# Two scalings spread over single steps: the Sinkhorn iteration of a three-layer kernel cut into 31 pieces, and the gates of two experts applied to their finished sums

## The chip, the cores and the metric

One core of one Trainium2 chip runs the whole program. The metric is the device time in microseconds (us) of one execution. The engines are named as the profile names them: PE is TensorE (matrix products), PEld its weight loads, DVE is VectorE, ACT is ScalarE, POOL is GpSimd, and SP is SyncE, which here only issues DMAs.

## The reference, cut to what matters

A linear attention layer gives `x` (3072 tokens of 384), a dense layer (384 to 2048 to 384) follows, and behind it a layer of 8 experts, each of which sees every token. The gates of the experts are not picked by top-k but by a Sinkhorn iteration over the whole 3072 x 8 table:

```
logits = x @ w_gate
P = exp(logits - logits.max())
for _ in range(8):
    P /= P.sum(1, keepdims=True) + 1e-09
    P /= P.sum(0, keepdims=True) + 1e-09
    P *= N / E
for e in range(E):
    h = np.maximum(x @ w1[e], 0.0)
    ye = h @ w2[e]
    out += P[:, e:e + 1] * ye
```

So no gate is known before the last token has its logits, and before 16 normalisations, each of which needs the whole table. A gate is one factor per token and expert; it may be applied to `h` or to `ye`, since the second product is linear.

## The kernel before, in words

The program has two parts. The first one (to about 771 us) holds attention, the dense layer and the first expert of one unit. The change lies at the beginning of the second part, which does the remaining work of the expert layer, and from there on all times are counted from the start of the span.

The second part works on three units of 1024 tokens, in the order 1, 2, 0. A unit passes through its experts one by one, each expert in four **steps** (`NGR = 4`) of 256 hidden columns. Unit 1 comes first and has all 8 experts, so step 0 to 3 is expert 0, step 4 to 7 is expert 1, step 8 begins expert 2. All weights and activations are split in a high and a low part, and every product is made in three passes of 128 x 512 matmuls (high x high, low x high, high x low).

**First products.** `x @ w1` of a step is done in Winograd's form: seven block products in place of eight (`TERMS`, in the order `ORDER = (0, 2, 1, 4, 3, 5, 6)`, positions k = 0 to 6). `first(s, a)` makes one of them, of 3 or 6 matmuls, in one PSUM bank, and `drain(s, a, ps)` adds it to what the others left (the tile `gt`; line 622 on DVE, but for the first one, which ACT copies, line 624). Five of the seven positions leave DVE one such sum; k = 4 leaves it two, and k = 0 none. There are only **two banks** for this, taken in turn by `next_ring`, so a first product waits until the sum of the bank's last user is done. Small results that pass through PSUM (named `sm`) take their turn in the same two banks.

**Between the products.** `weigh(s, z)` takes a finished block of `gt`. For the steps of expert 0 (`s < NGR`) ACT makes the relu, since the gates are not known yet; for later steps DVE makes relu and gate in one instruction (line 651, reading the gate tile `gp`). Then ACT makes the high part `gh`, and POOL (in unit 1) the low part `gl`.

**Second products.** `seconds(s)` makes the 36 matmuls of a step with `w2` (line 682). They are dealt out behind the first products of the next step, five behind each position, six behind the last, and add up in six banks through all experts of a unit. Expert 0 of unit 1 is kept apart: at its end `o_first` multiplies the six banks by the gate on DVE (line 697) and stores them to DRAM (`y0g`), to be added when the unit ends. So a step has 33 + 36 = 69 matmuls.

**Weights.** `make1` and `make2` convert the weights of a later step: four small sums on DVE, two copies on ACT, four subtractions on POOL, and DMAs.

**Sinkhorn.** The table `P` is the tile `lg`, 128 x 24 x 8. Row sums lie within a partition; column sums need a product with a matrix of ones on PE (line 377). The iteration is a list `sinks` of 11 entries, and three are called in each of the steps 0 to 2 (positions 1, 3, 5) and two in step 3 (positions 0, 2). A middle entry, `sink_next`, holds the PE product and all nine DVE instructions that follow it. The list is in hand-written order: what `side[k]` holds is issued behind the sum at position k and ahead of the five second products there.

**The first gates.** `gate_first` makes the gates of experts 0 and 1 of unit 1 without DRAM: eight ACT instructions put a gate column on a diagonal, two PE products with ones spread it over the partitions (line 582, the tile `pb`), and ACT copies it to `gp` (line 583). This is done at the end of step 3 and in step 4. `gate_out` writes all gates to DRAM (`ped`), and `gate_load` brings one expert's gates of a unit as a 128 x 1024 tile; there are two such tiles.

Of the kernel before, what the change touches and what calls it, by code (L numbers as in the profile page):

```python
# [8 lines left out]
F32 = mybir.dt.float32  # L9
# [12 lines left out]
E, F = 8, 1024  # L22
NTOK = B * S
# [61 lines left out]
def delta_mish_sinkhorn_kernel(  # L85
# [16 lines left out]
    nc = tc.nc  # L102
# [242 lines left out]
    P = lg  # L345
    Pf = lg.rearrange("p t e -> p (t e)")

    def sink_max():
        nc.vector.tensor_reduce(out=sk["m"][:, 0:1], in_=Pf, axis=AX.X, op=ALU.max)

    def sink_max_all():
        ps = small[0]()
        nc.tensor.transpose(ps[0:1, 0:128], sk["m"][:, 0:1], id_sb)
        nc.vector.tensor_reduce(out=sk["m"][0:1, 1:2], in_=ps[0:1, 0:128], axis=AX.X, op=ALU.max, negate=True)

    def sink_start():
        m2, m3 = sk["m"][0:1, 1:2], sk["m"][:, 2:3]
        ps2 = small[0]()[:, 0:1]
        mm(ps2, lhsT=sk["ones"][0:1, :], rhs=m2, start=True, stop=True)
        nc.vector.tensor_copy(m3, ps2)  # L360
        nc.scalar.activation(out=Pf, in_=Pf, func=AF.Sigmoid, bias=m3)
        d = sk["d"]
        nc.vector.tensor_scalar(out=d, in0=Pf, scalar1=-1.0, scalar2=1.0, op0=ALU.mult, op1=ALU.add)
        nc.vector.reciprocal(out=d, in_=d)
        nc.vector.tensor_tensor(out=Pf, in0=Pf, in1=d, op=ALU.mult)

    def sink_round():
        rs = sk["rs"]
        nc.vector.tensor_reduce(out=rs, in_=P, axis=AX.X, op=ALU.add)
        nc.vector.tensor_scalar(out=rs, in0=rs, scalar1=1e-9, scalar2=None, op0=ALU.add)  # L370
        nc.vector.reciprocal(out=rs, in_=rs)
        nc.vector.tensor_tensor(out=P, in0=P, in1=rs[:, :, None].to_broadcast([128, NT, E]), op=ALU.mult)
        nc.vector.tensor_reduce(out=sk["cs"], in_=P.rearrange("p t e -> p e t"), axis=AX.X, op=ALU.add)

    def sink_round_end():
        ps = small[0]()[:, 0:E]
        mm(ps, lhsT=sk["ones"], rhs=sk["cs"], start=True, stop=True)
        cr = sk["cr"]
        nc.vector.tensor_scalar(out=cr, in0=ps, scalar1=1e-9, scalar2=None, op0=ALU.add)
        nc.vector.reciprocal(out=cr, in_=cr)  # L380
        nc.vector.tensor_scalar(out=cr, in0=cr, scalar1=float(NTOK) / E, scalar2=None, op0=ALU.mult)
        nc.vector.tensor_tensor(out=P, in0=P, in1=cr[:, None, :].to_broadcast([128, NT, E]), op=ALU.mult)


    def sink_first():
        sink_start()
        sink_round()

    def sink_next():
        sink_round_end()  # L390
        sink_round()
# [150 lines left out]
    def gate_out():  # L542

        q = gq2[0]
        nc.scalar.activation(
            out=q[:, 0].rearrange("p (e t) -> p e t", e=E), in_=P.rearrange("p t e -> p e t"), func=AF.Copy
        )

        def turn():
            ps = small[0]()  # L550
            for a in range(2):
                nc.tensor.transpose(ps[0:96, a * 128:a * 128 + 128], q[:, 0, a * 96:a * 96 + 96], id_sb)
            rows = q[0:96, 1:3].rearrange("p a x -> p (a x)")[:, 0:256]
            nc.scalar.activation(out=rows, in_=ps[0:96, 0:256], func=AF.Copy)
            for a in range(2):
                nc.sync.dma_start(out=pe_dram[0][96 * a:96 * a + 96, :], in_=rows[:, 128 * a:128 * a + 128])

        return turn
# [9 lines left out]
    def gate_first():  # L568

        a = pool2[1, "x"].tile([128, 1024], F32, tag="x", name="gd")  # L570
        for e in range(2):
            pbs[U0, e] = pool2["p"].tile([128, 1024], F32, tag="p", name="gp")

        def diagonal(e):
            for t in range(8):
                nc.scalar.activation(
                    out=a[:, 128 * t:128 * t + 128], in_=id_sb, func=AF.Copy, scale=P[:, 8 * U0 + t, e:e + 1]
                )

        def spread_out(e, i):  # L580
            ps = next_ring("pb")
            mm(ps, lhsT=sk["ones"], rhs=a[:, 512 * i:512 * i + 512], start=True, stop=True)
            nc.scalar.activation(out=pbs[U0, e][:, 512 * i:512 * i + 512], in_=ps, func=AF.Copy)

        return diagonal, spread_out
# [1034 lines left out]
    with tc.manual_schedule():  # L1620
# [5 lines left out]
        for s in range(N + 1):  # L1626
# [18 lines left out]
            if s == NGR - 1:  # L1645
                diagonal, spread_out = gate_first()
                side[3].append(lambda: diagonal(1))
                for i in range(2):
                    side[5 + i].append(lambda i=i: spread_out(1, i))
            if s == NGR:  # L1650
                side[0].append(lambda: diagonal(0))
                for i in range(2):
                    side[1 + i].append(lambda i=i: spread_out(0, i))
                turn = []
                side[3].append(lambda: turn.append(gate_out()))
                side[5].append(lambda: turn[0]())
# [9 lines left out]
            if s > NGR and g == 1 and s + NGR - 1 < N:  # L1666
# [98 lines left out]
```

## Time and profile before

| what | value |
|---|---|
| median of 3 runs | 2259.17 us (2255.65 to 2260.9) |
| the profiled execution: its own time | 2261.18 us |
| its span, first to last instruction | 2259.2 us |
| mean granted PE clock | 0.972 of full speed |
| PE busy | 2185.5 us (97%) |
| DVE, ACT, POOL busy | 1408.2, 678.8, 680.1 us |

The page cuts the span in 40 slices of 56.5 us and gives for each the busy share of every engine in tenths, and the PE clock that the throttle granted, in tenths of full speed. One looks for slices in which a digit is lower than its neighbours, and then asks the trace for that stretch.

### The profile page before, as it was taken

To read this page: it belongs to the slowest core of one execution; us is meant where nothing else is said; L and a number is where in the kernel's file an instruction comes from. 1 tells how busy PE (TensorE), PEld (TensorE's weight loads), DVE (VectorE), ACT (ScalarE), POOL (GpSimd) and SP (SyncE) were. 2 spreads that over 40 slices of the span, in tenths; PEclk is the share of its full clock that TensorE was granted. 3 is DMA by queue.
4 is the path that set the end of the run, shared out by engine and by line. 5 is a ranking of instruction groups with operands and counts; after the bars stand their busy time and mean duration, and the time that the engine had idled before them with its cause. 6 is when DMAs were issued, how large, how long until landed. Compare 5 with 4: busy or idle time off the path is not lost.

```text
span 2259.2 us, 34766 instructions
## 1 busy us (share of the span) xinstructions
PE 2185.5 (97%) x14146; PEld 1801.7 (80%) x14146; DVE 1408.2 (62%) x2270; ACT 678.8 (30%) x1197; POOL 680.1 (30%) x532
## 2 busy tenths in 40 slices
PE   7788899999999989999999999999999999999998
PEld 6667788888888767888888888888888888888887
DVE  8894726373821376777777766666666666666665
ACT  6452332333333433333333322121121121211111
POOL 4504441435324546787786710000000000000000
PEclk7699999999999989999999999999999999999999
DMA  6385733544446325546556444444434444344342
GB/s 182 132 292 183 242 114 137 190 163 151 141 141 218 145 103 207 208 169 220 195 183 214 154 135 147 147 157 137 158 129 142 158 149 158 128 152 147 133 149 70
DMA packets 122222, 366.14 MB, mean 162 GB/s; under 512 B 9680, under 2 KB 50960, under 8 KB 121936
## 3 DMA queue, kind: packets, MB, share of 16 engines
q1 hardware_dynamic: 122064, 363.94, 47.5%
q8 instruction: 111, 1.82, 0.3%
q14 instruction: 47, 0.39, 0.1%
HBM read 271.53 MB, written 92.37 MB: 161 GB/s over the span
## 4 chain that ended last, share of the span: by engine, by line
PE 85%; DVE 10%; issue 2%; POOL 1%; ACT 1%; DMA 0%; SPq 0%; DVEq 0%; POOLq 0%; ACTq 0%
PE s L682 33%; PE b L615 30%; PE psh L310 8%; PE x L1263 7%; DVE t L1045 2%; DVE lane L1051 1%; PE y L334 1%; PE psa L982 1%; PE psa L1121 1%; DVE lane L1015 1%; PE psa L1285 1%; PE psa L1177 1%; DVE us L838 1%; PE psa L1087 1%; PE psa L1101 1%
## 5 line engine op out<-in xcount | busy, mean ns | idle before, releaser
L615 PE MATMUL b<-gx,gw 128*128 128x512 f32 x3036 | 798.0, 391 | 6.4 <-DVE gt L622 6.3
L622 DVE TENSOR_TENSOR gt<-b,gt 128x512 f32<-128x512 f32 x644 | 436.1, 689 | 443.6 <-PE b L615 421.1
L615 PEld LDWEIGHTS b<-gx,gw 128*128 128x128 f32 x3036 | 569.9, 188 | 127.0 <-DVE gt L622 8.1
L682 PE MATMUL s<-gh,gw 128*128 128x512 f32 x2208 | 624.0, 391 | 0.1
L657 ACT ACTIVATE gh<-gt 128x512 fp32r<-128x512 f32 x368 | 232.8, 633 | 971.0 <-DVE gt L651 969.9
L682 PEld LDWEIGHTS s<-gh,gw 128*128 128x128 f32 x2208 | 415.2, 188 | 88.4 <-issue 1.2
L682 PE MATMUL s<-gl,gw 128*128 128x512 f32 x1104 | 327.6, 392 | 0.0
L651 DVE SCALAR_TENSOR_TENSOR gt<-gt,gp 128x512 f32<-128x512 f32 x352 | 301.8, 857 | 4.9
L682 PEld LDWEIGHTS s<-gl,gw 128*128 128x128 f32 x1104 | 208.0, 189 | 43.5 <-issue 0.7
L310 PE MATMUL psh<-xh,w 128*128 128x512 f32 x672 | 224.0, 416 | 10.5 <-DVE gl L1252 8.2
L660 POOL TENSOR_TENSOR gl<-gt,gh 128x512 fp32r<-128x512 f32 x128 | 188.5, 1479 | 100.8 <-ACT gh L657 96.5
L660 DVE TENSOR_TENSOR gl<-gt,gh 128x512 fp32r<-128x512 f32 x240 | 164.6, 686 | 38.0 <-ACT gh L657 37.9
L1252 POOL TENSOR_TENSOR gl<-x,gh 128x512 fp32r<-128x512 f32 x80 | 103.1, 1289 | 261.0 <-ACT gh L1250 237.1
L310 PEld LDWEIGHTS psh<-xh,w 128*128 128x128 f32 x672 | 126.7, 196 | 43.2 <-DVE gl L1252 11.8
L1263 PE MATMUL x<-gh,w 128*128 128x512 f32 x576 | 153.0, 402 | 0.0
L540 POOL TENSOR_TENSOR gx<-gxr,gx 128x768 fp32r<-128x768 f32 x18 | 33.4, 1856 | 350.1 <-ACT gx L539 350.1
L471 POOL TENSOR_TENSOR gw<-gr,gw 128x640 fp32r<-128x640 f32 x70 | 116.1, 1661 | 68.7 <-ACT gw L481 68.7
L310 PE MATMUL psh<-xl,w 128*128 128x512 f32 x336 | 136.3, 406 | 0.4 <-DVE xl L838 0.4
L1263 PEld LDWEIGHTS x<-gh,w 128*128 128x128 f32 x576 | 109.0, 192 | 24.1 <-issue 1.4
L1244 ACT ACTIVATE x<-psh 128x512 f32<-128x512 f32 x80 | 47.9, 599 | 144.8 <-PE psh L310 138.8
L1263 PE MATMUL x<-gl,w 128*128 128x512 f32 x288 | 82.9, 397 | 1.0 <-POOL gl L1252 1.0
L310 PEld LDWEIGHTS psh<-xl,w 128*128 128x128 f32 x336 | 66.0, 196 | 16.1 <-DVE xl L838 1.3
(200 smaller groups left out, 2101.3 us busy)
## 6 DMA issues: line engine op xcount, KB each, us to landing
gw<-wg SPq DMA_DIRECT2D x57, 1280.0 KB, 8.4
w<-wd SPq DMA_DIRECT2D x88, 768.0 KB, 4.5
gw<-wg SPq DMA_DIRECT2D x57, 768.0 KB, 5.4
wg<-gw SPq DMA_DIRECT2D x29, 1280.0 KB, 6.0
wg<-gw SPq DMA_DIRECT2D x29, 768.0 KB, 5.1
wd<-w SPq DMA_DIRECT2D x24, 768.0 KB, 5.5
gr<-in_w_dram SPq DMA_DIRECT2D x35, 384.0 KB, 3.2
raw<-in_w_dram SPq DMA_DIRECT2D x35, 384.0 KB, 3.6
```

Source lines behind the costliest of these rows:

```text
L310: mm(ps, lhsT=wi(u, pw, kc), rhs=(xh, xl)[px][:, kc, :], start=(n == 0), stop=(n == 3 * KD - 1))
L471: nc.gpsimd.tensor_tensor(out=w[:, 1, lo:hi], in0=r, in1=w[:, 0, lo:hi].bitcast(F32), op=ALU.subtract)
L615: mm(ps, lhsT=w[:, pw, i * 128:i * 128 + 128], rhs=x[:, px, j, :], start=(n == 0), stop=(n == last))
L622: add = lambda o, i: nc.vector.tensor_tensor(out=t[:, o], in0=ps, in1=t[:, i], op=ALU.add)
L651: nc.vector.scalar_tensor_tensor(out=t, in0=t, scalar=0.0, in1=pbs[u, e][:, o:o + 512], op0=ALU.max, op1=ALU.mult)
L657: nc.scalar.activation(out=h, in_=t, func=AF.Copy)
L660: return lambda: eng.tensor_tensor(out=l, in0=t, in1=h.bitcast(F32), op=ALU.subtract)
L682: mm(o[3 * half + d], lhsT=w[:, pw, at:at + 128], rhs=hids[s, z][ph], start=(start and new and n == 0), stop=(end and not new and n == 2))
L1045: eng[0].tensor_tensor(out=slot[0], in0=lane[:, s + 1:32, s:s + 1].to_broadcast([128, n, s]), in1=lane[:, s:s + 1, 0:s].to_broadcast([128, ...
L1244: nc.scalar.activation(out=mi_x[u % 2], in_=hps.pop(u), func=AF.Mish)
L1252: eng.tensor_tensor(out=l, in0=p, in1=h.bitcast(F32), op=ALU.subtract)
L1263: mm(x2ps[c][k], lhsT=wo(u, pw, k * 128, k * 128 + 128), rhs=(h, l)[pg], start=(f == 0 and n == 0), stop=(f == U1 - 1 and n == 2))
```

## The change

The Sinkhorn list has 31 entries, each a pair: a PE part or nothing, and a part for DVE or ACT. One entry is called behind each first product, but for position 4 (which has two sums) and the very first position. The PE part is issued right behind the first product, ahead of its sum; the other part right behind the sum. A round is three entries: row sums, column sums, scaling.

The gates of experts 0 and 1 of unit 1 are no longer made by diagonals. The relu of the steps 0 to 7 is made by ACT. At the end of expert 0 the six banks are copied as they are to a tile `y2` (`o_plain`); in step 7 six DVE products apply gate 0 to it (`y_gate`); at the end of expert 1 its six banks are multiplied by gate 1 (`o_weighed`); in step 9 six DVE sums put both together (`y_sum`), and the result is stored to `y0g`. The gate tiles of both experts come from DRAM behind the last Sinkhorn entries, in step 5, and the gate of expert 2 is loaded in step 7. The loads and sums of the next unit's activations (`x_fetch`, `x_sums`, `x_split`) are placed 5 and 3 steps later in a unit.

```diff
+    def pe_columns():
+        held[:] = [small[0]()]
+        mm(held[0][:, 0:E], lhsT=sk["ones"], rhs=sk["cs"], start=True, stop=True)
...
-    sinks = deque([sink_max, sink_max_all, sink_first] + [sink_next] * (ROUNDS - 1) + [sink_round_end])
+    sinks = deque(
+        [(None, sink_max), (pe_max, sink_max_all), (pe_spread, sink_start), (None, sink_odds), (None, sink_odds_end)]
+        + [(None, sink_rows), (None, sink_columns), (pe_columns, sink_scale)] * ROUNDS
+    )
...
+    def gate_store():
+        rows = gq2[0][0:96, 1:3].rearrange("p a x -> p (a x)")[:, 0:256]
+        nc.scalar.activation(out=rows, in_=held[0][0:96, 0:256], func=AF.Copy)
+        for a in range(2):
+            nc.sync.dma_start(out=pe_dram[0][96 * a:96 * a + 96, :], in_=rows[:, 128 * a:128 * a + 128])
+        for e in range(2):
+            gate_load(U0, e)
+
+    sinks.extend([(None, gate_copy), (pe_gates, gate_store)])
...
-        if s < NGR:
+        if s < 2 * NGR:
             nc.scalar.activation(out=t, in_=t, func=AF.Relu)
...
-        start, end = s == begin2[u] or s == NGR, s == end2[u] or s == NGR - 1
+        start, end = s == begin2[u] or s in (NGR, 2 * NGR), s == end2[u] or s in (NGR - 1, 2 * NGR - 1)
...
-        o, put = os[u], o_first if s == NGR - 1 else o_out
+        o, put = os[u], {NGR - 1: o_plain, 2 * NGR - 1: o_weighed}.get(s, o_out)
...
+    def o_plain(u, half):
+        if not y2:
+            y2.append(pool2[1, "x"].tile([128, 2, KD, 1024], F32, tag="x", name="gy"))
         c = slice(512 * half, 512 * half + 512)
         for d in range(KD):
-            nc.vector.tensor_tensor(out=fin["y"][:, d, c], in0=os[u][3 * half + d], in1=pbs[u, 0][:, c], op=ALU.mult)
-        nc.sync.dma_start(out=y0g[0][:, :, c], in_=fin["y"][:, :, c])
+            if d == 1:
+                nc.vector.tensor_copy(y2[0][:, 0, d, c], os[u][3 * half + d])
+            else:
+                nc.scalar.activation(out=y2[0][:, 0, d, c], in_=os[u][3 * half + d], func=AF.Copy)
+
+    def y_gate(half, d):
+        c = slice(512 * half, 512 * half + 512)
+        tt(out=y2[0][:, 0, d, c], in0=y2[0][:, 0, d, c], in1=pbs[U0, 0][:, c], op=ALU.mult)
+
+    def o_weighed(u, half):
+        c = slice(512 * half, 512 * half + 512)
+        for d in range(KD):
+            tt(out=y2[0][:, 1, d, c], in0=os[u][3 * half + d], in1=pbs[u, 1][:, c], op=ALU.mult)
+
+    def y_sum(half, d):
+        c = slice(512 * half, 512 * half + 512)
+        tt(out=y2[0][:, 0, d, c], in0=y2[0][:, 0, d, c], in1=y2[0][:, 1, d, c], op=ALU.add)
+        if d == KD - 1:
+            nc.sync.dma_start(out=y0g[0][:, :, c], in_=y2[0][:, 0, :, c])
...
-            if s < NGR:
-                for k in (0, 2) if s == NGR - 1 else (1, 3, 5):
-                    side[k].append(sink_step)
...
+            if s in (2 * NGR - 1, 2 * NGR + 1):
+                fn = y_gate if s < 2 * NGR else y_sum
+                for half in range(2):
+                    for d in range(KD):
+                        side[(KD * half + d) // 2].append(lambda fn=fn, half=half, d=d: fn(half, d))
+                if s < 2 * NGR:
+                    side[3].append(lambda: gate_load(U0, 2))
...
-                    b = 6 + 10 * q
+                    b = 11 + 8 * q
...
-                z = drain(s, a, first(s, a))
+                ps = first(s, a)
+                item = sinks.popleft() if sinks and (s or k) and k != 4 else (None, None)
+                if item[0]:
+                    item[0]()
+                z = drain(s, a, ps)
+                if item[1]:
+                    item[1]()
```

In the order of instructions three places show it. The first is PE in step 1, around the first Sinkhorn product with ones (`sm`); `b` is the bank of a first product, `s` the banks of the second products. Before:

```order
L682 MATMUL s_7784<-gh,gw_7117 128x512
L615 MATMUL b_7800<-gx,gw_7118 128x512 x3
L377 MATMUL sm<-gate 128x8
L682 MATMUL s_7785<-gh,gw_7117 128x512
L682 MATMUL s_7783<-gl,gw_7117 128x512
```

After the change:

```order
L669 MATMUL s_7781<-gh,gw_7117 128x512
L602 MATMUL b_7810<-gx,gw_7118 128x512 x6
L389 MATMUL sm<-gate 128x8
L669 MATMUL s_7782<-gh,gw_7117 128x512
L669 MATMUL s_7783<-gh,gw_7117 128x512
```

The product with ones moved one position back, behind the first product of six matmuls at k = 2.

The second place is DVE in the same step, between two sums (`gt<-b`). Before, one sum is followed by all nine instructions of a `sink_next` and then by the next sum:

```order
L622 TENSOR_TENSOR gt<-b_7800,gt 128x512
L379 TENSOR_SCALAR gate<-sm 128x8
L380 RECIPROCAL gate<-gate 128x8
L381 TENSOR_SCALAR gate<-gate 128x8
L382 TENSOR_TENSOR lg<-lg,gate 128x192
L369 TENSOR_REDUCE gate<-lg 128x24
L370 TENSOR_SCALAR gate<-gate 128x24
L371 RECIPROCAL gate<-gate 128x24
L372 TENSOR_TENSOR lg<-lg,gate 128x192
L373 TENSOR_REDUCE gate<-lg 128x8
L622 TENSOR_TENSOR gt<-b_7821,gt 128x512
```

After the change the same nine kinds stand in three groups; here the last two of a round, with the sums of k = 1, 2 and 3 around them and two weight sums (`gr`) behind:

```order
L609 TENSOR_TENSOR gt<-b_7798,gt 128x512
L384 TENSOR_TENSOR lg<-lg,gate 128x192
L385 TENSOR_REDUCE gate<-lg 128x8
L609 TENSOR_TENSOR gt<-b_7810,gt 128x512
L393 TENSOR_SCALAR gate<-sm 128x8
L394 RECIPROCAL gate<-gate 128x8
L395 TENSOR_SCALAR gate<-gate 128x8
L396 TENSOR_TENSOR lg<-lg,gate 128x192
L494 TENSOR_TENSOR gr<-gr 128x128
L495 TENSOR_TENSOR gr<-gr 128x256
L609 TENSOR_TENSOR gt<-b_7835,gt 128x512
```

At most four Sinkhorn instructions now stand between two sums.

The third place is DVE from the end of step 8 through position 3 of step 9. Before (a gated block, an activation sum `gxr`, then the sums of k = 1 and 2):

```order
L651 SCALAR_TENSOR_TENSOR gt<-gt,gp 128x512
L531 TENSOR_TENSOR gxr<-gxr 128x256
L622 TENSOR_TENSOR gt<-b_8900,gt 128x512
L622 TENSOR_TENSOR gt<-b_8914,gt 128x512
L651 SCALAR_TENSOR_TENSOR gt<-gt,gp 128x512
L490 TENSOR_TENSOR gr<-gr 128x128
L491 TENSOR_TENSOR gr<-gr 128x256
L622 TENSOR_TENSOR gt<-b_8933,gt 128x512
```

After the change, from the three products that empty the second half of expert 1's banks:

```order
L698 TENSOR_TENSOR gy<-s_8356,gp 128x512
L698 TENSOR_TENSOR gy<-s_8357,gp 128x512
L698 TENSOR_TENSOR gy<-s_8358,gp 128x512
L702 TENSOR_TENSOR gy<-gy 128x512 x2
L609 TENSOR_TENSOR gt<-b_8885,gt 128x512
L702 TENSOR_TENSOR gy<-gy 128x512 x2
L609 TENSOR_TENSOR gt<-b_8902,gt 128x512
L638 SCALAR_TENSOR_TENSOR gt<-gt,gp 128x512
L702 TENSOR_TENSOR gy<-gy 128x512 x2
L494 TENSOR_TENSOR gr<-gr 128x128
L495 TENSOR_TENSOR gr<-gr 128x256
L609 TENSOR_TENSOR gt<-b_8924,gt 128x512
```

Nine more instructions of 128 x 512 stand there, ahead of the sum of position 3.

## Rows read from the trace of the kernel before

**Rows 1.** The page: the granted PE clock in 40 slices.
```profile
PEclk7699999999999989999999999999999999999999
```
**Rows 2.** What PE waited for, 771 to 875 us: total, times, longest.
```profile
PE b L615 <- DVE gt L622: 6.3, 4, 4.2
PE sm L377 <- DVE gt L622: 3.7, 3, 2.2
```
**Rows 3.** Busy time by engine in steps 1, 3, 4, 6 and 8.
```profile
core 0: us, PE busy (x) PEld busy (x) DVE busy (x) ACT busy (x) POOL busy (x), PEclk, DMA share, GB/s
784.06:809.65 25.59, 19.99 (x76) 15.36 (x75) 17.56 (x43) 8.14 (x12) 7.76 (x6) 0.87 0.00 1
...
831.17:853.19 22.02, 19.86 (x79) 15.24 (x77) 13.06 (x29) 11.33 (x22) 11.78 (x10) 0.92 0.41 150
853.19:871.24 18.05, 18.01 (x76) 13.71 (x75) 10.12 (x17) 9.12 (x20) 8.85 (x7) 1.00 0.39 140
886.88:902.52 15.64, 15.64 (x70) 12.95 (x69) 11.01 (x16) 5.03 (x7) 10.97 (x9) 1.00 0.79 269
918.16:933.80 15.64, 15.64 (x70) 12.96 (x69) 12.89 (x17) 5.03 (x7) 11.08 (x9) 1.00 0.52 185
```
**Rows 4.** PE in order of time, around the starts of steps 1 and 5.
```profile
782.57 2.33 PE L615 MATMUL b<-gx,gw 128*128 128x512 f32 x9 [0.42 <-DVE gt L622]
...
790.20 1.12 PE L615 MATMUL b<-gx,gw 128*128 128x512 f32 x3 [4.16 <-DVE gt L622]
...
871.24 0.84 PE L615 MATMUL b<-gx,gw 128*128 128x512 f32 x3
```
**Rows 5.** A stretch of 2 us behind that wait; columns as in Rows 3.
```profile
792.00:794.00 2.00, 2.00 (x6) 1.71 (x7) 1.86 (x6) 0.00 (x0) 0.82 (x1) 0.50 0.00 0
```
**Rows 6.** The chain that ended last, pieces between 838 and 870 us.
```profile
840.63 0.12 PE sm L377 x2
840.75 1.26 PE s L682 x5
...
843.39 1.13 PE s L682 x5
...
847.70 0.86 PE pb L582 x2
...
867.26 0.22 PE sm L552 x2
```
**Rows 7.** DVE in order of time: Sinkhorn rounds beside POOL, and alone.
```profile
806.15 0.16 DVE L379 TENSOR_SCALAR gate<-sm 128x8 f32<-128x8 f32 x1
...
807.23 1.40 DVE L382 TENSOR_TENSOR lg<-lg,gate 128x192 f32<-128x192 f32 x1
...
811.97 0.68 DVE L622 TENSOR_TENSOR gt<-b,gt 128x512 f32<-128x512 f32 x1
...
822.30 0.16 DVE L379 TENSOR_SCALAR gate<-sm 128x8 f32<-128x8 f32 x1
...
822.93 0.36 DVE L382 TENSOR_TENSOR lg<-lg,gate 128x192 f32<-128x192 f32 x1
...
825.09 0.28 DVE L492 TENSOR_TENSOR gr<-gr 128x128 f32<-128x128 f32 x1
```
**Rows 8.** POOL in order of time, the same stretch.
```profile
807.12 1.30 POOL L660 TENSOR_TENSOR gl<-gt,gh 128x512 fp32r<-128x512 f32 x1
```
**Rows 9.** Groups by shape, 871 to 1262 us: busy us, mean ns.
```profile
L651 DVE SCALAR_TENSOR_TENSOR gt<-gt,gp 128x512 f32<-128x512 f32 x100 | 119.2, 1192 | 2.6
...
L697 DVE TENSOR_TENSOR gy<-s,gp 128x512 f32<-128x512 f32 x3 | 1.9, 676 | 0.0
```
**Rows 10.** Gate tiles by DMA: us from issue to landing, min, median, max.
```profile
DMA to landing us min/median/max: 4.0/9.0/10.5
```
**Rows 11.** ACT in order of time: the gate table's copy.
```profile
862.19 0.56 ACT L545 ACTIVATE gq<-lg 128x192 f32<-128x192 f32 x1
```

More of the change, by code (lines that the diff above doesn't have):

```diff
@@ L346, in delta_mish_sinkhorn_kernel, with pe_max @@
     Pf = lg.rearrange("p t e -> p (t e)")
+    rs, d = sk["rs"], lambda: sk["d"]
+    held = []
+    tt, ts1 = nc.vector.tensor_tensor, nc.vector.tensor_scalar
     def sink_max():
         nc.vector.tensor_reduce(out=sk["m"][:, 0:1], in_=Pf, axis=AX.X, op=ALU.max)
+    def pe_max():
+        held[:] = [small[0]()]
+        nc.tensor.transpose(held[0][0:1, 0:128], sk["m"][:, 0:1], id_sb)
     def sink_max_all():
-        ps = small[0]()
-        nc.tensor.transpose(ps[0:1, 0:128], sk["m"][:, 0:1], id_sb)
@@ L354, in sink_max_all, with pe_spread @@
-        nc.vector.tensor_reduce(out=sk["m"][0:1, 1:2], in_=ps[0:1, 0:128], axis=AX.X, op=ALU.max, negate=True)
+        nc.vector.tensor_reduce(out=sk["m"][0:1, 1:2], in_=held[0][0:1, 0:128], axis=AX.X, op=ALU.max, negate=True)
+    def pe_spread():
+        held[:] = [small[0]()]
+        mm(held[0][:, 0:1], lhsT=sk["ones"][0:1, :], rhs=sk["m"][0:1, 1:2], start=True, stop=True)
     def sink_start():
-        m2, m3 = sk["m"][0:1, 1:2], sk["m"][:, 2:3]
-        ps2 = small[0]()[:, 0:1]
-        mm(ps2, lhsT=sk["ones"][0:1, :], rhs=m2, start=True, stop=True)
@@ L360, in sink_start, with sink_odds @@
-        nc.vector.tensor_copy(m3, ps2)
+        m3 = sk["m"][:, 2:3]
+        nc.vector.tensor_copy(m3, held[0][:, 0:1])
         nc.scalar.activation(out=Pf, in_=Pf, func=AF.Sigmoid, bias=m3)
[L362 to L368, printed above, removed]
+    def sink_odds():
+        ts1(out=d(), in0=Pf, scalar1=-1.0, scalar2=1.0, op0=ALU.mult, op1=ALU.add)
+        nc.vector.reciprocal(out=d(), in_=d())
@@ L369, in sink_round, with sink_odds_end, sink_rows, sink_columns @@
+    def sink_odds_end():
+        tt(out=Pf, in0=Pf, in1=d(), op=ALU.mult)
+    def sink_rows():
         nc.vector.tensor_reduce(out=rs, in_=P, axis=AX.X, op=ALU.add)
-        nc.vector.tensor_scalar(out=rs, in0=rs, scalar1=1e-9, scalar2=None, op0=ALU.add)
+        ts1(out=rs, in0=rs, scalar1=1e-9, scalar2=None, op0=ALU.add)
         nc.vector.reciprocal(out=rs, in_=rs)
-        nc.vector.tensor_tensor(out=P, in0=P, in1=rs[:, :, None].to_broadcast([128, NT, E]), op=ALU.mult)
+    def sink_columns():
+        tt(out=P, in0=P, in1=rs[:, :, None].to_broadcast([128, NT, E]), op=ALU.mult)
@@ L373, in sink_round, with sink_scale @@
         nc.vector.tensor_reduce(out=sk["cs"], in_=P.rearrange("p t e -> p e t"), axis=AX.X, op=ALU.add)
-    def sink_round_end():
-        ps = small[0]()[:, 0:E]
-        mm(ps, lhsT=sk["ones"], rhs=sk["cs"], start=True, stop=True)
+    def pe_columns():
+        held[:] = [small[0]()]
+        mm(held[0][:, 0:E], lhsT=sk["ones"], rhs=sk["cs"], start=True, stop=True)
+    def sink_scale():
         cr = sk["cr"]
-        nc.vector.tensor_scalar(out=cr, in0=ps, scalar1=1e-9, scalar2=None, op0=ALU.add)
+        ts1(out=cr, in0=held[0][:, 0:E], scalar1=1e-9, scalar2=None, op0=ALU.add)
@@ L380, in sink_round_end @@
         nc.vector.reciprocal(out=cr, in_=cr)
[L381 to L391, printed above, removed]
-    sinks = deque([sink_max, sink_max_all, sink_first] + [sink_next] * (ROUNDS - 1) + [sink_round_end])
-    def sink_step():
-        if sinks:
-            sinks.popleft()()
+        ts1(out=cr, in0=cr, scalar1=float(NTOK) / E, scalar2=None, op0=ALU.mult)
@@ L400, in delta_mish_sinkhorn_kernel @@
+        tt(out=P, in0=P, in1=cr[:, None, :].to_broadcast([128, NT, E]), op=ALU.mult)
+    sinks = deque(
+        [(None, sink_max), (pe_max, sink_max_all), (pe_spread, sink_start), (None, sink_odds), (None, sink_odds_end)]
+        + [(None, sink_rows), (None, sink_columns), (pe_columns, sink_scale)] * ROUNDS
+    )
     NGR = U2 // 2
@@ L540, in x_split, with gate_copy, pe_gates @@
         nc.gpsimd.tensor_tensor(out=x[:, 1, s, o], in0=r[:, s], in1=x[:, 0, s, o].bitcast(F32), op=ALU.subtract)
-    def gate_out():
-        q = gq2[0]
+    def gate_copy():
         nc.scalar.activation(
-            out=q[:, 0].rearrange("p (e t) -> p e t", e=E), in_=P.rearrange("p t e -> p e t"), func=AF.Copy
+            out=gq2[0][:, 0].rearrange("p (e t) -> p e t", e=E), in_=P.rearrange("p t e -> p e t"), func=AF.Copy
         )
[L549 to L558, printed above, removed]
+    def pe_gates():
+        held[:] = [small[0]()]
+        for a in range(2):
+            nc.tensor.transpose(held[0][0:96, a * 128:a * 128 + 128], gq2[0][:, 0, a * 96:a * 96 + 96], id_sb)
+    def gate_store():
+        rows = gq2[0][0:96, 1:3].rearrange("p a x -> p (a x)")[:, 0:256]
+        nc.scalar.activation(out=rows, in_=held[0][0:96, 0:256], func=AF.Copy)
+        for a in range(2):
+            nc.sync.dma_start(out=pe_dram[0][96 * a:96 * a + 96, :], in_=rows[:, 128 * a:128 * a + 128])
+        for e in range(2):
+            gate_load(U0, e)
+    sinks.extend([(None, gate_copy), (pe_gates, gate_store)])
     def gate_load(u, e):
@@ L566, in gate_load @@
         pbs[u, e] = pb
[L568 to L585, printed above, removed]
     ring, ringn = [], [0]
@@ L690, in delta_mish_sinkhorn_kernel @@
     fin, slot = {}, [0]
-    def o_first(u, half):
-        if half not in fin and not fin:
-            fin["y"] = pool2[1, "x"].tile([128, KD, 1024], F32, tag="x", name="gy")
+    y2 = []
+    def o_plain(u, half):
+        if not y2:
+            y2.append(pool2[1, "x"].tile([128, 2, KD, 1024], F32, tag="x", name="gy"))
         c = slice(512 * half, 512 * half + 512)
         for d in range(KD):
-            nc.vector.tensor_tensor(out=fin["y"][:, d, c], in0=os[u][3 * half + d], in1=pbs[u, 0][:, c], op=ALU.mult)
-        nc.sync.dma_start(out=y0g[0][:, :, c], in_=fin["y"][:, :, c])
+            if d == 1:
[14 more added lines that the diff above has]
+            nc.sync.dma_start(out=y0g[0][:, :, c], in_=y2[0][:, 0, :, c])
     def o_open(u):
@@ L1641, in delta_mish_sinkhorn_kernel @@
             side = {k: [] for k in range(7)}
-            if s < NGR:
-                for k in (0, 2) if s == NGR - 1 else (1, 3, 5):
-                    side[k].append(sink_step)
[L1645 to L1656, printed above, removed]
+            if s in (2 * NGR - 1, 2 * NGR + 1):
[5 more added lines that the diff above has]
+                    side[3].append(lambda: gate_load(U0, 2))
             for n, make, lo, hi in ((s + 2, make1, 0, NW1), (s + 1, make2, NW1, GW)):
@@ L1665, in delta_mish_sinkhorn_kernel @@
                     side[1 - (make is make2)].append(lambda n=n, lo=lo, hi=hi: again(n, lo, hi))
-            if s > NGR and g == 1 and s + NGR - 1 < N:
+            if s > 2 * NGR and g == 1 and s + NGR - 1 < N:
                 side[5].append(lambda: gate_load(*plan[s + NGR - 1][0:2]))
```

## The prediction

> **What bounds the kernel now.** The first view is the profile page's line of the granted clock [rows 1]. From slice 3 on every slice shows 9 but one, slice 15, about 790 to 847 us: there the second part begins, and there PE waits long enough to lose its clock. The view of waits says for whom: 6.3 us of first products and 3.7 us of Sinkhorn products wait for DVE's sums [rows 2]. The table by step shows what a step is worth. Step 6 takes 15.64 us with PE busy all of it, so a step's 69 matmuls cost 15.64/69 = 0.227 us each, and DVE is busy for 11.01 us of it. Steps 1, 3 and 4 take 25.59, 22.02 and 18.05 us [rows 3]. Step 5 begins at 871.24 us; step 1 begins with the seventh of the nine matmuls at 782.57, at 784.06 [rows 4]. The four steps of the Sinkhorn iteration thus take 871.24 - 784.06 = 87.18 us where 4 x 15.64 = 62.56 would do: **24.6 us are there to be had**. Everything else of the second part is bound by PE.
>
> Where do the 24.6 us go? PE idles 25.59 - 19.99 = 5.6 us in step 1 and 2.2 in step 3 [rows 3]; the longest wait is 4.16 us [rows 4], and the stretch behind it runs at a granted clock of 0.50, the lower of the two levels, 1.2 GHz [rows 5]. A mean clock of 0.87 over 25.59 us costs 3.3 us, one of 0.92 over 22.02 costs 1.8 [rows 3]. Four spreads `pb` take 0.86 us each, 3.4 in all; a Sinkhorn product takes 0.12 us and makes the five matmuls behind it last 1.26 in place of 1.13, so 0.25 each, 2.0 for eight [rows 6]. The cause of the waits is one queue: nine DVE instructions stand ahead of the next sum, with two banks for the first products. They last 825.09 - 822.30 = 2.8 us alone, but 811.97 - 806.15 = 5.8 us beside a busy POOL [rows 7].
>
> **The change, part by part.**
>
> *Sinkhorn in pieces.* Two rounds per step stay, in steps 1 to 4. Take position 1 and 2. Behind the three matmuls of k = 1 come the sum (0.68 us [rows 7]) and the two column instructions, a good quarter of the round's 2.8, some 0.8 us. PE asks for their result 5 + 6 matmuls later, 11 x 0.227 = 2.5 us; 0.9 us are left over. The next first product needs the sum of k = 2: PE gets there 0.25 + 1.13 = 1.4 us later, the sum needs 0.7. So both waits vanish while DVE's instructions run at their own length, and the new order costs only its two products, 0.5 us per step.
>
> They don't always run at their own length. Instruction L382 takes 0.36 us alone and 1.40 us when a POOL subtraction runs from 807.12 for 1.30 us; it ends just behind it [rows 7, 8]. DVE's load is the check: step 6 less its four gated blocks (ACT makes the relu now) is 11.01 - 4 x 1.19 = 6.2 us [rows 3, 9], and two rounds are 5.6 to 11.6. That is 11.8 to 17.8 us in a step of 15.64 + 0.5 = 16.1. Between the ends POOL decides, which is busy for 10.97 of 15.64 us [rows 3]; at the middle, 14.8, DVE keeps up on the whole. I take 0.25 us per step for a product with ones that comes a little late, bounds 0 and 1.7. Steps 1 to 4: 4 x (15.64 + 0.5 + 0.25) = 65.6 us, against 87.18: **21.6 us gained**.
>
> The relu moves 4 ACT instructions per step into steps 4 to 7; ACT is busy for 5.03 us of 15.64 [rows 3], so this is hidden by two thirds of the step.
>
> *Step 0* does the same work before and after, with the two small products one position later or earlier; DVE's waits there stay of one kind. I take no change, bounds plus and minus 1 us.
>
> *The spreads* are gone with their 16 diagonals (counted in the 87.18). In their place the two gate transposes of 0.22 us [rows 6] move to position 1 of step 5, where they wait for the gate table's copy, 0.56 us on ACT [rows 11], which now stands behind two of the bank copies and the copy of the step's first product. PE reaches it 2.5 us into the step; I take 0.7 us of wait, bounds 0 and 1.5. **0.9 us lost.** The bank copies themselves have the cover that `o_first` has now: PE needs the first half's banks 9 second products and 9 first ones later, 4 us, for copies on two engines.
>
> *The gate loads.* SP waits for the table's store before it issues two loads, and the conversions' DMAs wait behind; the weights they bring are needed a step later. The loads land in 4.0 to 10.5 us [rows 10], with nearly two steps to `y_gate`. The gate of expert 2 is tighter: its tile is free when `y_gate` ends, about 10 us into step 7, and 9.0 us later it has landed, 3.4 us into step 8; the first gated block wants it at about 6. With 10.5 it is 5. I take 0; where it comes later than about 8, PE waits for what is over.
>
> *Step 7* has six `y_gate`. Not one like it (two SBUF inputs, 128 x 512) is in the trace; between L697 from PSUM, 0.68, and the gated blocks, 1.19 [rows 9], they are 4.1 to 7.1 us. DVE: 6.2 + 7.1 = 13.3 of 15.64 at most. Six of them and two weight sums stand ahead of the sum of k = 3, which has less than 3 us of slack: 0.5 us, bounds 0 and 1.5.
>
> *Step 8* empties expert 1's banks as step 4 did expert 0's, and has the load of 12.89 us that step 8 has now without loss [rows 3]. 0.
>
> *Step 9* is the worst: 11.01 us, three bank products of 0.68 and six `y_sum` of 0.68 to 1.19 are 17.1 to 20.2 us in 15.64. Nearly all of the new work lies ahead of the sum of k = 3. The excess is 1.5 to 4.5 us, and where PE gets most of it as one wait, the clock may fall behind it as it fell behind the 4.16 us. I take 3.0, bounds 1 and 6.5. What the step is late, the next ones give back to DVE, whose load is 11 again.
>
> Here a rule of the Trainium skill speaks against the change. The page "SBUF — State Buffer", section "SBUF: two separate sides", says that VectorE and GpSimd share a pair of ports as an exclusive lock, held for the whole instruction, which a DVE instruction with two SBUF inputs must have. L382 agrees: 1.40 us beside POOL's 1.30. By that rule step 9 would need POOL's 10.97 and ten locked DVE instructions of 0.68 one behind the other, 17.8 us, 2.1 over the step; with that in place of the 3.0 the sum below would be 18.1.
>
> *The activation sums* move out of steps 7 to 10; a step with one of them loses nothing now (step 8, 15.64 us [rows 3]). 0.
>
> **The sum.** 21.6 - 0.9 - 0.5 - 3.0 = **17.2 us**. The profiled execution took 2261.18 us, so the same after the change is 2244.0; the median of the runs is 2.0 us lower, and **2242 us** is what I predict for it.
>
> **The rivals.**
>
> *Nothing waits.* If POOL's and DVE's instructions happen to miss each other, steps 1 to 4 take 64.6 us, and steps 5, 7 and 9 lose about 1.5: 21 us, 2238. For it: a round alone is 2.8 us. Against it: POOL's 10.97 us per step.
>
> *The lock makes DVE the bound.* Rounds of 5.8 us throughout: 17.8 us per step, 6.8 us lost in steps 1 to 4, step 9 at its upper end with the clock (6.5), step 7 at 1.5, step 5 at 0.9: 22.6 - 15.7 = 7 us, 2252. For it: four instructions of each round take the slow form when POOL has a backlog. Against it: the two forms share the rounds of the trace, and the load there was the same.
>
> *Slower: the product with ones.* It stands in PE's in-order queue twice per step, ahead of five or six second products that need nothing from it. If the column sums come late by w in each of 8 rounds, PE idles 8w, and the clock loses about as much again (5.6 us idle and 3.3 us of clock in step 1). The gain of 22.6 - 4.4 = 18.2 is gone at w = 1.4 us with w x 0.6 of clock; at w = 2.2 us the waits cost 28 us, 10 more than the gain, 2269. Against it: 0.9 us of slack in each, and one lock costs 1.0.
>
> **How the numbers follow.** Forecast 0.68, by itself 2238 to 2247; nothing waits 0.14; DVE the bound 0.13; slower 0.05. The range from 2236 to 2250 leaves out the slower case, the upper half of the DVE case and little at the lower end. What a measurement of this kernel can tell from no change is about 0.2%, 4.5 us (the three runs spread over 5.3): faster 0.92, same 0.04 (the worst of the DVE case and the edge of the slower one), slower 0.04.
>
> **What would show it.** Right: slice 15 of the clock at 9; steps 1 to 4 at 16.0 to 16.8 us each; the waits for DVE's sums down from 10 us to 3 or less up to step 5; step 9 at 17 to 20 us with the wait at position 4 or 5, behind k = 3's sum. Wrong: Sinkhorn products that wait in most rounds for the column sums, a granted clock of 0.5 anywhere in steps 1 to 4, a wait in step 8 for the gate's DMA, or step 9 at 15.64.

## The result and the profile after

The changed kernel takes 2238.4 us (median of 4 runs, 2237.6 to 2240.5) where the kernel before took 2260.0 beside it. The ratio is 0.9905 (95% interval 0.9883 to 0.9927), a gain of 21.6 us. The prediction was 2242 us, the range 2236 to 2250.

The granted clock on the profile page of the changed kernel, 40 slices, answers to [rows 1]:

```profile
PEclk8699999999999999999999999999999999999999
```

Slice 15 is at 9 now. What PE waited for from 764 to 960 us (steps 0 to 9; total, times, longest) answers to [rows 2]:

```profile
PE b L602 <- DVE gt L609: 3.1, 4, 1.6
PE sm L389 <- DVE gate L385: 1.0, 4, 0.2
```

The busy time by step, steps 1 to 6 and 9, answers to [rows 3]; its columns are the same:

```profile
777.67:794.37 16.70, 16.47 (x74) 13.31 (x74) 13.95 (x31) 8.40 (x13) 9.82 (x8) 1.00 0.00 0
794.37:811.22 16.85, 16.61 (x75) 13.25 (x73) 14.21 (x30) 7.48 (x12) 10.24 (x9) 1.00 0.47 173
811.22:828.08 16.86, 16.62 (x75) 13.25 (x73) 14.22 (x30) 7.56 (x12) 10.25 (x9) 1.00 0.46 173
828.08:844.91 16.83, 16.59 (x74) 13.24 (x73) 14.21 (x31) 8.03 (x13) 10.25 (x9) 1.00 0.48 171
844.91:861.15 16.24, 16.10 (x72) 13.04 (x71) 7.41 (x14) 8.96 (x16) 10.01 (x9) 1.00 0.76 249
861.15:876.79 15.64, 15.64 (x70) 12.96 (x69) 6.45 (x12) 7.44 (x12) 10.14 (x9) 1.00 0.50 184
908.07:926.30 18.23, 16.23 (x71) 12.80 (x69) 18.05 (x27) 5.03 (x7) 11.95 (x8) 1.00 0.68 245
```

Steps 1 to 4 take 67.2 us in place of 87.2, at the full clock throughout. Behind them step 5 is 0.6 us longer than a bare step (15.64), and step 9 is the only long one: DVE is busy for 18.05 of its 18.23 us. There PE waits twice, for the sums of positions 1 and 3, in its order of time:

```profile
914.79 1.65 PE L602 MATMUL b<-gx,gw 128*128 128x512 f32 x6 [0.44 <-DVE gt L609]
...
920.95 1.65 PE L602 MATMUL b<-gx,gw 128*128 128x512 f32 x6 [1.56 <-DVE gt L609]
```

**Two gains, not one.** Step 0 of the kernel before starts at 771.63 us of its profiled execution and step 10 at 949.44: 177.8 us. In the changed kernel PE's order of time shows, for the first matmuls of steps 0 and 10:

```profile
764.98 0.62 PE L602 MATMUL b<-gx,gw 128*128 128x512 f32 x2
...
926.30 0.84 PE L602 MATMUL b<-gx,gw 128*128 128x512 f32 x3
```

That is 161.3 us, **16.5 us less**. The spans differ by 2259.2 - 2235.7 = 23.5. Of this, 771.6 - 765.0 = 6.6 us lie ahead of step 0, in code that the change doesn't touch, and 0.4 behind step 10. What those 6.6 us are is the first question of the experiments.

### The profile page after: what moved, and what is told of

The parts are those of the page before. It is cut to its first block, busy times and chain, and to the rows that moved or that the text cites. A ratio compares the mean times of both kernels' runs of the same rounds, so it can differ in the third digit from the quotient of the medians.

```text
span 2235.7 us, 34754 instructions
## 1 busy us (share of the span) xinstructions
PE 2171.5 (97%) x14138; PEld 1792.3 (80%) x14138; DVE 1399.6 (63%) x2268; ACT 684.3 (31%) x1197; POOL 680.4 (30%) x532
## 4 chain that ended last, share of the span: by engine, by line
PE 86%; DVE 10%; issue 1%; POOL 1%; ACT 1%; DMA 0%; SPq 0%; DVEq 0%; POOLq 0%; ACTq 0%
PE s L669 33%; PE b L602 30%; PE psh L310 8%; PE x L1269 7%; DVE t L1051 2%; DVE lane L1057 2%; PE y L334 1%; PE psa L988 1%; PE psa L1127 1%; PE psa L1291 1%; DVE lane L1021 1%; PE psa L1183 1%; PE psa L1149 1%; DVE us L844 1%; PE psa L1093 1%
## 5 line engine op out<-in xcount | busy, mean ns | idle before, releaser
L638 DVE SCALAR_TENSOR_TENSOR gt<-gt,gp 128x512 f32<-128x512 f32 x336 | 274.9, 818 | 4.5
L310 PEld LDWEIGHTS psh<-xl,w 128*128 128x128 f32 x336 | 65.6, 195 | 16.2 <-DVE xl L844 1.3
```

What stands on the lines that cost most here:

```text
L310: mm(ps, lhsT=wi(u, pw, kc), rhs=(xh, xl)[px][:, kc, :], start=(n == 0), stop=(n == 3 * KD - 1))
L638: nc.vector.scalar_tensor_tensor(out=t, in0=t, scalar=0.0, in1=pbs[u, e][:, o:o + 512], op0=ALU.max, op1=ALU.mult)
```

## The experiments

But for the activation loads and sums, which now come in later steps, the change lies in steps 0 to 10, and behind these all traces agree to 0.5 us. So each run is read by step from its trace: from the start of step 0 to that of step 10 before takes 177.8 us and the changed kernel 161.3.

**The kernel before, again.** No edit.

> The kernel before, unchanged, for its first part. In the two profiles the second part began at 771.6 us (before) and 765.0 us (after), though no line of the first part changed. If that is chance of the execution (the granted clock of the first 300 us), this third profile may begin its second part anywhere between 764 and 773 us. If it belongs to the program, it begins within 1 us of 771.6. From the first matmul of step 0 to the first one of step 10 both expect 177.8 us, as in the profile of before (949.4 - 771.6).

The start of its second part, in PE's order of time:

```profile
777.77 0.61 PE L615 MATMUL b<-gx,gw 128*128 128x512 f32 x2
```

So 6 us later than in the first profile of the same kernel, and from there to step 10 it takes 177.5 us. Over the eleven profiles of this study (both kernels twice, seven variants; the first part is the same in all) step 0 starts between 764.0 and 780.0 us, and the steps agree to 0.3 us wherever their code does. That range is wider than the 764 to 773 us that were expected of chance, but the same kernel shows both 771.6 and 777.8: the 6.6 us ahead of step 0 are chance of the execution.

**One part undone: Sinkhorn in its old groups.** The gates stay as in the change.

```diff
-    sinks = deque(
-        [(None, sink_max), (pe_max, sink_max_all), (pe_spread, sink_start), (None, sink_odds), (None, sink_odds_end)]
-        + [(None, sink_rows), (None, sink_columns), (pe_columns, sink_scale)] * ROUNDS
-    )
+    start = [pe_spread, sink_start, sink_odds, sink_odds_end, sink_rows, sink_columns]
+    middle = [pe_columns, sink_scale, sink_rows, sink_columns]
+    groups = deque([[sink_max], [pe_max, sink_max_all], start] + [middle] * (ROUNDS - 1) + [[pe_columns, sink_scale]])
...
+            if s < NGR:
+                for k in (0, 2) if s == NGR - 1 else (1, 3, 5):
+                    side[k].append(group_step)
```

> The changed kernel with one part undone: Sinkhorn again in 11 groups in steps 0 to 3, at the old places, while the gates are applied as in the change. Theory (the queue of nine instructions ahead of the next sum): the waits return, step 1 about 25.6 us, step 2 about 21.5, step 3 about 20.3 (22.0 without its two spreads of 0.86), step 4 back at 15.7; from the start of step 0 to that of step 5 about 95 us where the change has 79.9, a time near 2254 us. Rival (the gain came from the spreads, the diagonals and the gated blocks that left DVE): within 4 us of the change, 84 us at most for that stretch.

Busy time by step, steps 1 to 5:

```profile
785.13:810.70 25.57, 20.05 (x76) 15.36 (x76) 17.58 (x43) 8.17 (x12) 7.83 (x6) 0.87 0.00 1
810.70:832.15 21.45, 18.81 (x76) 14.59 (x75) 17.45 (x39) 7.33 (x11) 10.20 (x9) 0.92 0.37 135
832.15:852.35 20.20, 18.02 (x75) 14.45 (x73) 13.11 (x29) 7.92 (x12) 11.56 (x10) 0.92 0.39 144
852.35:867.99 15.64, 15.64 (x71) 12.95 (x69) 6.68 (x13) 8.41 (x14) 9.89 (x9) 1.00 0.52 184
867.99:884.39 16.40, 16.11 (x72) 13.03 (x71) 6.72 (x12) 9.11 (x16) 10.19 (x9) 1.00 0.74 247
```

All steps are where the theory put them, waits and half clock with them; the run's 2261.6 us, where about 2254 were expected, holds a late start of the second part, 772.75. Steps 0 to 9 take 176.8 us. So the pieces are worth 176.8 - 161.3 = 15.5 us, 8.9 of them in step 1, and everything done to the gates 177.8 - 176.8 = 1.0: the spreads give back 4.2 (1.8 in step 3, 2.4 in step 4), steps 5 and 9 take 3.4, and the rest is 0.1 in steps 1 and 2, and rounding.

**What the 1.2 us over a bare step are.** Two kernels ask it. The first leaves out the eight products with ones:

```diff
-        ts1(out=cr, in0=held[0][:, 0:E], scalar1=1e-9, scalar2=None, op0=ALU.add)
+        ts1(out=cr, in0=sk["cs"], scalar1=1e-9, scalar2=None, op0=ALU.add)
...
-        + [(None, sink_rows), (None, sink_columns), (pe_columns, sink_scale)] * ROUNDS
+        + [(None, sink_rows), (None, sink_columns), (None, sink_scale)] * ROUNDS
```

> The changed kernel without the eight products with ones: the scaling reads the column sums of its own partition, so the sum over partitions is left out. Steps 1 to 4 take 16.84 us in the change, 1.2 over the 15.64 of a bare step. Theory: all of it is the products, their own cost and their wait for late column sums, so these steps fall to 15.64 to 15.8 us, 4.5 us in all. Rival (DVE as the bound, sums late for their banks): the steps stay above 16.3 us, since DVE's work is the same.

Steps 1 to 4 take 15.70, 15.64, 15.64 and 15.64 us. Step 2:

```profile
795.76:811.40 15.64, 15.64 (x71) 12.95 (x69) 13.64 (x30) 7.50 (x12) 10.35 (x9) 1.00 0.50 185
```

With nearly the same DVE work, and POOL as busy, the sums are never late for their banks. (Step 5 takes 17.0: PE now comes to the transposes of the gate table sooner than the table is copied, and waits 0.9 us for ACT.)

The second leaves POOL idle:

```diff
+        if NS2 <= n < 8:
+            return
...
+        if s < 6:
+            hids[s, z] = h, h
+            return lambda: None
```

> The changed kernel with POOL idle in steps 0 to 5: the low parts of the activations there aren't made (the high part is used in their place) and the low parts of the weights of steps 3 to 7 are left as they were. Theory (POOL holds up the column multiplication, which takes 1.1 to 1.4 us in place of 0.36, and so the product with ones comes late): the multiplication takes 0.36 us in all rounds and steps 1 to 4 fall from 16.84 to 16.1 to 16.3 us; what stays is the products' own cost of 0.25 us each. Rival (the product's cost is its own, whatever POOL does): the steps stay at 16.7 to 16.9 us.

The busy time of step 3, and DVE's order of time in step 2 (the sum of position 5, the column multiplication, the column sum):

```profile
817.71:833.84 16.13, 16.13 (x74) 13.40 (x73) 10.40 (x30) 7.55 (x12) 0.00 (x0) 1.00 0.49 179
```

```profile
813.81 0.69 DVE L611 TENSOR_TENSOR gt<-b,gt 128x512 f32<-128x512 f32 x1 [1.14 <-PE b L604]
814.42 0.35 DVE L384 TENSOR_TENSOR lg<-lg,gate 128x192 f32<-128x192 f32 x1
814.80 0.54 DVE L385 TENSOR_REDUCE gate<-lg 128x8 f32<-128x192 f32 x1
```

The same place in the changed kernel, DVE, POOL and PE:

```profile
806.88 0.69 DVE L609 TENSOR_TENSOR gt<-b,gt 128x512 f32<-128x512 f32 x1 [1.19 <-PE b L602]
807.49 1.43 DVE L384 TENSOR_TENSOR lg<-lg,gate 128x192 f32<-128x192 f32 x1
808.95 0.51 DVE L385 TENSOR_REDUCE gate<-lg 128x8 f32<-128x192 f32 x1
```

```profile
807.41 1.30 POOL L647 TENSOR_TENSOR gl<-gt,gh 128x512 fp32r<-128x512 f32 x1
```

```profile
807.76 1.52 PE L602 MATMUL b<-gx,gw 128*128 128x512 f32 x6
809.52 0.39 PE L389 MATMUL sm<-gate 128*128 128x8 f32 x2 [0.24 <-DVE gate L385]
809.76 0.93 PE L669 MATMUL s<-gh,gw 128*128 128x512 f32 x3
```

In the second round of each step, this one, the column multiplication meets POOL's subtraction and takes 1.43 us in place of 0.35; the column sum ends at 809.46, and PE, through with its six matmuls at 807.76 + 6 x 0.227 = 809.12, waits for it. The first round of step 2, DVE and PE, is late too, by too little for the view of waits:

```profile
797.74 1.12 DVE L384 TENSOR_TENSOR lg<-lg,gate 128x192 f32<-128x192 f32 x1
798.90 0.52 DVE L385 TENSOR_REDUCE gate<-lg 128x8 f32<-128x192 f32 x1
```

```profile
798.00 1.52 PE L602 MATMUL b<-gx,gw 128*128 128x512 f32 x6
799.47 0.39 PE L389 MATMUL sm<-gate 128*128 128x8 f32 x2
```

Here the multiplication takes 1.12 us, the column sum ends at 799.42, and PE is through at 799.36. By the distance of the matmuls around it, the first product of such a step costs 0.46 us and the second 0.74, together the 1.2 us over a bare step. Of the eight rounds only the first, in step 1, has a multiplication that is hardly held up (0.46 us), and a product that costs no more than its own.

Without POOL a step costs 16.13 - 15.64 = 0.49 us more than a bare one, 0.245 per product; POOL costs the other 0.7.

**The product issued late.** The same arithmetic, PE's product behind the second products of its position and the scaling behind the next first product:

```diff
+                if behind:
+                    behind.popleft()()
...
+                swap = item[0] is pe_columns
...
+                if swap:
+                    item[0]()
+                    behind.append(item[1])
```

> The changed kernel with the product with ones issued behind the five or six second products of its position, and the scaling behind the next first product. Theory: the column sums are there 1.1 to 1.4 us ahead of the product then, so each product costs its own 0.25 us and steps 1 to 4 fall from 16.84 to about 16.15 us, 2.7 us in all; step 5 may lose some of it, since the gate table is ready one position later. About 2 us below the change. Rival (the price is the product itself and its weight load, not a wait): the steps stay at 16.6 or above.

Steps 1 to 4 take 16.05 to 16.24 us. Step 2, and the column multiplication of its second round:

```profile
792.79:808.92 16.13, 16.13 (x76) 13.39 (x75) 13.04 (x29) 7.55 (x12) 10.25 (x9) 1.00 0.50 180
```

```profile
805.80 1.43 DVE L384 TENSOR_TENSOR lg<-lg,gate 128x192 f32<-128x192 f32 x1
```

POOL is as busy as ever, the multiplication of the second round as slow, and nobody waits for it. (That of the first round isn't held up any more: 0.36 us in steps 2 to 4.) Step 5 takes 16.75 (16.24 in the change): the table is ready later, and PE waits 0.5 us for its copy. In all 159.2 us against 161.3; 2239.1 us median of 6, ratio 0.9924 (0.9906 to 0.9942).

**The expert sums spread.** Two of the six in each of steps 9, 10 and 11:

```diff
+            if 2 * NGR < s <= 2 * NGR + 3:
+                for n in range(2):
+                    i = 2 * (s - 2 * NGR - 1) + n
+                    side[(0, 5)[n]].append(lambda i=i: y_sum(i // KD, i % KD))
```

> The changed kernel with the six sums of the two experts spread over steps 9, 10 and 11, two each, at positions 0 and 5. Theory (DVE overloaded in step 9 alone): step 9 falls from 18.2 to 15.64 us and steps 10 and 11 stay at 15.64, 2.6 us below the change. Rival (emptying expert 1's banks, or the first gated blocks, are the cause): step 9 stays above 17 us.

Steps 9, 10 and 11 take 15.64 us each; step 9:

```profile
914.84:930.48 15.64, 15.64 (x70) 12.95 (x69) 14.79 (x22) 5.03 (x7) 12.43 (x9) 1.00 0.49 185
```

From step 0 to 10: 158.7 us; 2241.4 us median of 6, ratio 0.9922 (0.9908 to 0.9936).

**Is step 9 too much for DVE, or is it POOL?** The spreading doesn't tell. This kernel keeps all six sums in step 9 and leaves POOL idle in steps 8 to 10, by the same edit as above.

> The changed kernel with POOL idle in steps 8 to 10: the low parts of the activations aren't made there, and the low parts of the weights of steps 9 to 12 are left as they were. It asks what lengthens step 9 from 15.64 to 18.23 us. Theory (the lock: a pair of expert sums takes 1.3 us alone, and 2.7, 1.5 and 1.3 beside POOL): all three pairs take 1.3 us, and the sum of position 3 ends about 10.4 us into the step, when PE wants its bank, so step 9 takes 15.7 to 16.1 us. Rival (DVE's own work is too much for the step, whatever POOL does): step 9 stays above 17.4 us.

The three pairs of sums in step 9, DVE's order of time, in the changed kernel:

```profile
911.46 2.67 DVE L702 TENSOR_TENSOR gy<-gy 128x512 f32<-128x512 f32 x2
...
914.66 1.49 DVE L702 TENSOR_TENSOR gy<-gy 128x512 f32<-128x512 f32 x2
...
917.39 1.28 DVE L702 TENSOR_TENSOR gy<-gy 128x512 f32<-128x512 f32 x2
```

With POOL idle, the pairs and the step:

```profile
917.32 1.28 DVE L708 TENSOR_TENSOR gy<-gy 128x512 f32<-128x512 f32 x2
...
919.12 1.28 DVE L708 TENSOR_TENSOR gy<-gy 128x512 f32<-128x512 f32 x2
...
921.65 1.29 DVE L708 TENSOR_TENSOR gy<-gy 128x512 f32<-128x512 f32 x2
```

```profile
914.66:930.30 15.64, 15.64 (x70) 12.95 (x69) 14.13 (x26) 5.02 (x7) 0.00 (x0) 1.00 0.63 220
```

15.64 us, a little under the 15.7 to 16.1 expected: DVE has room for all of it, 14.13 us, when POOL doesn't hold it up. With POOL busy and two sums in the step, as in the run before, nothing waits either. So it takes both, six sums in one step and POOL beside them; DVE's own work alone isn't too much.

**All three together, and the change again on the same chip.** Late product, spread sums, and an empty entry ahead of the gate table's transposes:

```diff
-    sinks.extend([(None, gate_copy), (pe_gates, gate_store)])
+    sinks.extend([(None, gate_copy), (None, None), (pe_gates, gate_store)])
```

> The changed kernel with the product with ones issued late, the sums of the two experts spread, and the transposes of the gate table one position later. If all three costs are what the theory says, steps 1 to 4 take 16.15 us, step 5 about 15.9 (16.24 in the change), step 9 15.64: 2.7 + 0.4 + 2.6 = 5.7 us below the change, so a ratio to the kernel before of about 0.988. If the costs are elsewhere, within 2 us of the change.

> The changed kernel again, on the same chip as the three variants, for their comparison and for its first part. 2238 us, ratio 0.990. If the start of the second part is chance of the execution, it may lie anywhere between 764 and 773 us here; if it belongs to the program, within 1 us of 765.0. From the first matmul of step 0 to that of step 10 both expect 161.3 us.

Steps 2, 5 and 9 of the kernel with all three:

```profile
808.74:824.87 16.13, 16.13 (x76) 13.40 (x75) 13.03 (x29) 7.55 (x12) 10.25 (x9) 1.00 0.50 180
857.25:873.29 16.04, 16.04 (x73) 13.22 (x72) 7.13 (x16) 9.71 (x16) 10.76 (x9) 1.00 0.64 237
920.21:935.85 15.64, 15.64 (x71) 12.95 (x69) 14.79 (x22) 5.03 (x7) 12.43 (x9) 1.00 0.50 185
```

From step 0 to 10 it takes 155.85 us, the change again 161.4 (161.3 in its first profile): 5.55 us, of the 5.7 expected. The medians of 6 runs are 2237.7 (2232.8 to 2247.2) and 2242.9 us (2241.1 to 2249.5), the ratios to before 0.9911 (0.9891 to 0.9931) and 0.9933 (0.9917 to 0.9949). The intervals overlap, and the 0.988 expected of the first isn't reached: the start of the second part wanders by more than 5 us over the runs (780.0 and 776.65 us in these two profiles, where 773 at most was expected of the second). The stretch itself tells them apart: there this version beats both kernels. That its median is lower too is within the noise.

## Why the prediction was right

| term | predicted, us | measured, us |
|---|---|---|
| steps 1 to 4, from 87.2 | 65.6 | 67.2 |
| step 0 | 0 | +0.3 |
| step 5, over 15.64 | 0.9 | 0.6 |
| step 7 | 0.5 | 0.0 |
| step 8 | 0 | 0.0 |
| step 9 | 3.0 | 2.6 |
| gain | 17.2 | 16.5 |

*The mechanism* held in the main. What stands ahead of the next sum in DVE's queue was the cause: old groups with new gates lose 15.5 of the 16.5 us, wait by wait and with the half clock. The waits up to step 5 fell from 10 to 2.1 us (3.1 + 1.0, less 2.0 in step 9), where 3 or less was named. But "one queue: nine DVE instructions" isn't the cause of the longest wait, 4.16 us, nor of the half clock behind it, 3.3 us in that step. That sum stood behind the iteration's start, `sink_first`. In the kernel before, ACT and DVE:

```profile
783.86 1.28 ACT L361 ACT_TABLE_LOAD   x1
```

```profile
785.64 0.26 DVE L363 TENSOR_SCALAR gq<-lg 128x192 f32<-128x192 f32 x1 [3.06 <-ACT lg L361]
785.94 1.35 DVE L364 RECIPROCAL gq<-gq 128x192 f32<-128x192 f32 x1
```

DVE sat idle for 3.06 us, as ACT first made the blocks of step 0 and loaded a table. The cut into pieces puts sums between there too, so the forecast of the gain wasn't touched. How much of the other waits is the nine instructions' own 2.8 us and how much POOL's part of the 5.8 wasn't run: no kernel has the old groups with POOL idle.

*The sum* agreed to 0.7 us partly by luck: steps 0 to 4 were 1.9 us worse than forecast, and steps 5, 7 and 9 together 1.2 better.

*The product with ones* was priced right, 0.25 against 0.245 us. Its **lateness was mis-sized**: "0.25 us per step for a product with ones that comes a little late" is 0.7, inside the bounds of 0 and 1.7. The slack of 0.9 us was worked out at position 1 and 2, for instructions at their own length. The round at positions 5 and 6 meets POOL every time, 1.1 us of delay, and is late in all four steps; the one at positions 1 and 2 meets it in three of them, 0.8 us of delay, and is late by a little. So one of the named signs of a wrong forecast, products that wait in most rounds, came, in seven of eight, at a price too small to decide anything; and steps 2 to 4, with 16.83 to 16.86 us, lie just above the 16.0 to 16.8 named. The slower rival needed 1.4 us of lateness in every round; the worst was 0.4.

*DVE as the bound*, the rival of 2252, did not come: DVE is busy for 14.2 of 16.85 us, near the 14.8 taken for the middle.

*Step 5*'s 0.6 us is made otherwise than forecast (0.2 for the transposes, 0.7 of wait): with the transposes a position later the step is still 0.4 us over 15.64, which leaves 0.2 of wait.

*Step 9* was right in place and size: its waits, 0.44 and 1.56 us on PE, stand behind the sums of positions 1 and 3. But the sum for it took DVE's load from rows in which POOL already holds DVE up, as if it were DVE's own work. The run with POOL idle shows that the work fits, and the run with spread sums that POOL does no harm there without the six. By the rule of the Trainium skill's page "SBUF — State Buffer", section "SBUF: two separate sides", the prediction's estimate from rows was 2.1 us over the step; 2.6 were measured, and none with POOL idle. The same page of the Trainium skill, section "Who interferes with whom", says which instructions take the shared ports: those with two SBUF inputs and some one-input forms do, reductions don't. The rows agree: 1.43 against 0.35 us for the multiplication, 0.51 to 0.54 for the column sum with POOL or without.

*The gates* came without any wait: the gate of expert 2 wasn't waited for in step 8, which took 15.64 us. *Step 7*'s six products took 0.67 to 1.57 us each, 6.1 in all, inside the 4.1 to 7.1 named, and hid wholly. That "not one like it" is in the trace was an oversight. The units behind unit 1 make their low parts on DVE, an instruction of that shape from two SBUF tiles. On the page of the kernel before:

```profile
L660 DVE TENSOR_TENSOR gl<-gt,gh 128x512 fp32r<-128x512 f32 x240 | 164.6, 686 | 38.0 <-ACT gh L657 37.9
```

Its 0.69 us on the mean give the lower bound.

*The median* moved by 21.6 us, 4.4 more than predicted. In the profiled pair the steps moved by 16.5 and what lies behind them by 0.4; the rest, 6.6 us, lies in the first part, by chance. That it is so in the other executions isn't shown, as they have no trace. But in the later comparison, with 6 and 11 runs, the difference of the medians is 2257.9 - 2242.9 = 15.0 us.

## What to carry to other kernels

A small serial computation beside a matmul pipeline cost little here (1.2 us per step, 0.5 with the late product) once no more of it stood between two bank sums than the slack of the two banks; cutting it finer than "one round" did nearly all of the work, 15.5 of 16.5 us, not moving it off the engine. Put a product that waits for a slow engine behind the independent matmuls of its place, not ahead of them: 0.7 us per step for a change of order. And read each step's stretch from the trace when the whole time wanders: 5.55 us showed there, where two traces of one kernel agree to 0.3, and were within the noise of the medians.

## What the runs showed of the hardware that was not expected

The start of the second part, after the same code, wandered from 764.0 to 780.0 us between executions, 0.7% of the whole time, while 160 us of dense work behind it repeated to 0.3 us. It goes with PE's granted clock from the span's start to step 0, here the earliest start (the late product) and the latest (all three together):

```profile
0.00:764.00 764.00, 706.60 (x7674) 585.49 (x7674) 431.66 (x787) 297.50 (x596) 300.91 (x264) 0.95 0.54 179
0.00:780.00 780.00, 725.92 (x7673) 600.15 (x7674) 427.26 (x787) 297.54 (x596) 300.67 (x264) 0.91 0.52 175
```

PE is busy 19 us longer with the same matmuls. Of the other nine starts, those up to 767.4 us had 0.94, those from 771.5 to 772.8 had 0.93, and the last two, 776.7 and 777.8, had 0.91 and 0.92. What decides the clock in an execution stays open.
